# A list-scheduling planner for an FNet-plus-MLP kernel: a model of TensorE's half clock, unused products in planned gaps, and a table of urgencies for the work ahead of the MLP

## The chip, the cores and the metric

One core of a Trainium2 chip runs the kernel. The time is the device time of one execution in microseconds (us), the median of three runs. The profile is that of one further execution.

## The reference

The input x is 2048 tokens by 1024 channels (f32). With six rows sa, ca, ga, sb, cb, gb of 1024 values made from a condition vector (`silu(c) @ w_mod`):

```
h = layernorm(x) * (1 + ca) + sa
x = x + ga * Real(DFT_seq(DFT_hidden(h)))          # spectral part
h = layernorm(x) * (1 + cb) + sb
x = x + gb * (gelu(h_n @ w1 + b1) @ w2 + b2)       # h_n: h, layer-normalised again; w1 1024x3584, w2 3584x1024
```

The DFT matrices are inputs as well. Products must be good to f32, so operands are split into a high and a low f16 part and multiplied in three passes.

## The kernel before

**Spectral part.** The tokens are normalised in 16 tiles (`ln1`), transposed on TensorE (PE, L2740), and folded on VectorE (DVE: L2757 to L2827) with the symmetries of the DFT, which halves the products. ScalarE (ACT, L2833) and DVE (L2835) split the folded operand. The hidden transform is a set of units (`hid_unit`, PE L3060) for two classes of operands; ACT and DVE (L2586, L2589) split each result, and L2589 splits the sequence matrices too. The sequence transform runs over eight blocks b of 256 tokens (`seq_pair`): a product Q (PE L3136), evicted by ACT (L3140), and a product P (PE L3124), evicted by DVE in two halves (L3145, L3150).

**Per block, between the two parts** (`ln2`): DVE multiplies by ga (L3267), a DMA on GpSimd's (POOL) queue adds x from DRAM (L3277, L2180), ACT squares (L3241), DVE normalises (L3296, L3300), small DVE steps make a root (L2673 to L2676, L3307), ACT writes the normalised rows (L3309). Then `z_psum`: 20 transposes on PE (L3490), ACT and DVE split seven combinations into f16 (L3511, L3538), and ten small PE products (L3498) add or subtract earlier combinations in PSUM. L3538's results of blocks 4 and 5 go to DRAM on POOL's queue (L3530). Blocks 6 and 7 are "held": only L3267 is done at once, and the rest (`z_held`) during the MLP. There are 20 transposes and 10 products for each of the blocks 0 to 5.

**MLP.** Both weight products use a scheme with seven products in place of eight (Strassen-like), so a group is seven times 12 matmuls of 512 columns. The first product is L3962 (2352 matmuls in all), the second L4089 (2352). The first two groups of L3962 (`gemm3_first`, 168 matmuls) need only blocks 0 to 3, so they may stand between the last spectral steps. The weights are scaled and split on the fly by ACT (L2434) and DVE (L2447, L2461); `need` and `emitted` force what a group needs ahead of it.

**The planner.** Nothing is ordered by hand. The program is made of tasks, each with an engine, a cost in us and dependences, in streams; each stream has a due time. While the program is written, the planner keeps one clock for each engine, starts in each step the task that can start now and is due first (`pick_first`), and writes its instructions. So costs, lags (`LAGS`: from one engine's end to another's start), landing times of DMAs (`LANDS`) and due times settle the order on every engine, and the hardware then runs each engine's queue in that order. Up to the last combination of block 5 PE's products are planned too (`in_order`); after it PE's order is the MLP's fixed sequence, and the rest is placed around it. A PSUM bank is reused by a list of the tasks that last used it (`last`, `zlast`, `bank_used`).

Of the kernel before, what the change touches and what calls it, by code (L numbers as in the profile page):

```python
# [17 lines left out]
P = 128  # L18
# [1973 lines left out]
def fast(ctx, tc, x, cre, cim, dre, dim, w1, b1, w2, b2, c, wm, out):  # L1992
# [207 lines left out]
    LAGS = {"w": 2.0, "rowl": 1.0, "crawl": 0.5, "row": 0.2, "rowp": 3.0, "ld": 0.5, "z": 1.0, "s": 0.5, "u": 0.3, "op": 0.4, "comb": 0.3, "ln": 0.2}  # L2200

    LANDS = {"dma": 2.0, "st": 4.0, ("st", "d"): 7.0, ("st", "u"): 5.0, ("st", "s"): 4.0, ("st", "z"): 4.0, ("st", "xa"): 8.0}
# [11 lines left out]
    class Task:  # L2214
        def __init__(self, eng, cost, fn, deps=(), key=None):
# [3 lines left out]
            self.tag, self.due, self.lag = None, 0.0, LAT  # L2219

# [43 lines left out]

    def chain(*steps):
# [5 lines left out]

    def push(stream, tag, tasks, due=0.0):
        for t in tasks:
            t.tag, t.due, t.lag = tag, due, LAGS.get(f"{stream}l" if t.eng == "dma" else stream, LAGS.get(stream, LAT))
            streams.setdefault(f"st_{stream}" if t.eng == "st" else stream, deque()).append(t)
# [228 lines left out]
    def add(stream, eng, cost, fn, deps=(), key=None, due=0.0, tag=None):  # L2504
        t = Task(eng, cost, fn, deps, key)
        push(stream, tag or stream, [t], due)
# [91 lines left out]
    def mod_part(k):  # L2598
# [10 lines left out]
        add("modp", "pe", CP * (1 + (k == 0)), f, [("wm", k)], ("mp", k), 1.0)  # L2609
# [72 lines left out]
    def ln1(bt):  # L2682
# [50 lines left out]
        for j in range(2):  # L2733
            for ga_, gd_, base in ((0, 3, 0), (1, 2, 1)):
# [3 lines left out]
                def turn(g, bk, j=j):  # L2738
# [7 lines left out]
                    add("lnt", "pe", 0.55, lambda g=g, bk=bk, turn=turn: turn(g, bk), deps + last[s], None, due)  # L2746
# [18 lines left out]
    def special(cls):  # L2765
# [4 lines left out]
        for hb in range(2):  # L2770
# [5 lines left out]
            k = add("lnt", "pe", 0.6, turn, [("n", 8 * cls + 7), *last[s]], None, due)  # L2776
# [148 lines left out]
    def row(n, j):  # L2925
# [4 lines left out]
        for c_ in range(2):  # L2930
# [34 lines left out]
            add("rowp", "pe", 2 * CP, f, deps, ("wrr", m), due)  # L2965
# [74 lines left out]
    def hid_unit(tp, t, cls, c_):  # L3040
# [23 lines left out]
        bp = 1024 * s  # L3064
        deps += last[s]
        last[s] = [("hid", n)]
        due = 40.0 + 22.0 * cls
        key = add("hidp", "pe", 2.1, f, deps, ("hidp", n), due)
# [31 lines left out]
    def seq_pair(b):  # L3100
# [37 lines left out]
        add("seqp", "pe", 2.75, q_mm, ak[tp] + copk + bank_deps + ([("qs", b - 1)] if b else []), ("Q", b), due)  # L3138
        add("seqp", "pe", 3.0, p_mm, ak[tp] + copk + bank_deps + ([("y", b - 1)] if b else []), ("P", b), due)
        ev = lambda: act.activation(qv(b, 0, (257, 2), (1, 256)), PA(qb, (256, 2), (1, 256)), AF.Copy)  # L3140
        add("qs", "act", 0.65, ev, [("Q", b), ("qsz", b % 2)] + ([("y", b - 2)] if b > 1 else []), ("qs", b), due)
# [1312 lines left out]
```

## Time and profile before

| what | value |
|---|---|
| median of three runs | 1337.07 us (1335.74 to 1341.33) |
| the profiled execution: its time, its span | 1336.37 us, 1334.6 us |
| PE, DVE, ACT, POOL busy | 1228.5, 1058.8, 741.8, 253.9 us |
| mean granted clock of TensorE | 0.964 |
| first product of the MLP starts | 274.91 us |
| last combination of block 5 ends, from there on nothing but the MLP | about 305 us |

The span runs from the first instruction to the last; the run's own time is 1.8 us longer. PE busy counts a running matmul, at whatever clock; "granted clock" is 1 at full speed and 0.5 at half. A row of the timeline gives start, duration, engine, line, operation, output and inputs, and in brackets the engine's idle time before it with what ended it. `arena` is the one large SBUF tile and `ps` the eight PSUM banks, so most rows have the same names and go by their lines.

### The profile page before, as it was taken

How to read it: one execution, taken by the hardware profiler on the slowest of the kernel's cores; microseconds unless marked ns; L12 is line 12 of the kernel's file. 1: busy time of each engine (PE TensorE's matmuls, PEld its weight loads, DVE VectorE, ACT ScalarE, POOL GpSimd, SP SyncE). 2: the span in 40 equal slices, each digit the busy share in tenths (PEclk: the TensorE clock that was granted, in tenths of full speed). 3: DMA queues.
4: the chain of work that ended last, by engine and by line, in shares of the span. 5: the costliest groups of instructions: out<-in, count | busy, mean ns of one | idle time of the engine just before them, and what ended most of it. 6: DMA issues, size and time to landing. Idle time of an engine off the chain costs nothing.

```text
span 1334.6 us, 16823 instructions
## 1 busy us (share of the span) xinstructions
PE 1228.5 (92%) x5909; PEld 575.7 (43%) x5909; DVE 1058.8 (79%) x1602; ACT 741.8 (56%) x1194; POOL 253.9 (19%) x382
## 2 busy tenths in 40 slices
PE   3669796869999999999999999999999999999996
PEld 1225454534444444444444444444444444444442
DVE  5788688866888989989999986566777868585884
ACT  4875547766787585666746451466455554536330
POOL 2000033222000001000011101545233332233101
PEclk9779688889999999999999999999999999999998
DMA  9998378798436365543629696999585766575155
GB/s 364 402 298 268 111 244 214 173 262 278 170 113 231 107 247 175 196 156 111 251 89 291 162 394 170 292 271 331 200 298 176 270 240 190 199 280 195 60 177 114
DMA packets 105704, 292.59 MB, mean 219 GB/s; under 512 B 13340, under 2 KB 13356, under 8 KB 103688
## 3 DMA queue, kind: packets, MB, share of 16 engines
q1 hardware_dynamic: 77032, 198.26, 42.4%
q0 software_dynamic: 28576, 93.15, 24.3%
q8 instruction: 48, 0.79, 0.2%
q14 instruction: 48, 0.39, 0.1%
HBM read 205.37 MB, written 90.18 MB: 221 GB/s over the span
## 4 chain that ended last, share of the span: by engine, by line
PE 69%; DVE 6%; issue 2%; ACT 2%; DMA 1%; POOL 0%; SPq 0%; DVEq 0%; POOLq 0%
PE ps L3962 34%; PE ps L4089 34%; DVE arena L2447 2%; DVE arena L4141 1%; ACT arena L2434 1%; DMA fw<-arena 1%; DVE arena L2461 1%; DVE arena L3538 0%; DVE arena L3988 0%; ACT arena L3981 0%; PE ps L3387 0%; ACT arena L3511 0%; DVE arena L3296 0%; DVE arena L3375 0%; DVE arena L4196 0%
## 5 line engine op out<-in xcount | busy, mean ns | idle before, releaser
L3962 PE MATMUL ps<-arena 128*128 128x512 f16 x2352 | 514.6, 381 | 7.8 <-DVE arena L3150 6.6
L4089 PE MATMUL ps<-arena 128*128 128x512 f16 x2352 | 511.7, 379 | 5.9 <-DVE arena L4141 5.4
L3962 PEld LDWEIGHTS <-arena 128*128 128x128 f16 x2352 | 231.0, 98 | 287.9 <-issue 13.2
L4089 PEld LDWEIGHTS <-arena 128*128 128x128 f16 x2352 | 230.0, 98 | 284.4 <-issue 7.6
L4141 DVE SCALAR_TENSOR_TENSOR arena<-ps,i4c,arena 128x1024 f32<-128x1024 f32 x179 | 229.2, 1280 | 79.5 <-PE ps L4089 78.3
L2434 ACT ACTIVATE arena<-arena,shc 128x512 f16<-128x512 f32 (+1 forms) x115 | 116.2, 1016 | 119.4 <-DVE arena L2461 67.0
L2447 DVE SCALAR_TENSOR_TENSOR arena<-arena,shc 128x512 f16<-128x512 f32 (+1 forms) x115 | 128.9, 1121 | 39.1 <-ACT arena L2434 38.9
L3846 ACT ACTIVATE arena<-arena 128x512 f32<-128x512 f32 (+4 forms) x159 | 97.3, 613 | 111.7 <-DVE arena L3855 91.1
L2461 DVE TENSOR_TENSOR arena<-arena 128x512 f32<-128x512 f32 (+1 forms) x196 | 149.4, 764 | 4.0
L3981 ACT ACTIVATE arena<-arena,b1s,i1c 128x512 f32<-128x512 f32 x78 | 63.4, 813 | 86.4 <-DVE arena L3988 86.4
L2434 ACT ACTIVATE arena<-arena,s1c 128x512 f16<-128x512 f32 (+1 forms) x70 | 60.6, 886 | 65.2 <-DVE arena L2461 33.5
L3855 DVE TENSOR_TENSOR arena<-arena 128x256 f32<-128x256 f32 x240 | 88.4, 419 | 3.6 <-DMA arena<-in_cre_dram 3.0
L3988 DVE TENSOR_TENSOR arena<-arena,ps 128x512 f32<-128x512 f32 x78 | 53.3, 684 | 43.2 <-PE ps L3962 41.9
L3627 POOL PARTITION_ALL_REDUCE sums<-sums x21 | 11.5, 552 | 373.3 <-DVE sums L3623 355.2
L2447 DVE SCALAR_TENSOR_TENSOR arena<-arena,s1c 128x512 f16<-128x512 f32 (+1 forms) x70 | 65.9, 960 | 10.0 <-ACT arena L2434 9.6
L3984 ACT ACTIVATE arena<-ps 128x512 f32<-128x512 f32 x78 | 45.9, 589 | 39.0 <-PE ps L3962 38.7
L2447 DVE SCALAR_TENSOR_TENSOR arena<-arena,s2c 128x1024 f16<-128x1024 f32 x49 | 61.7, 1279 | 2.9 <-ACT arena L2434 2.8
L2434 ACT ACTIVATE arena<-arena,s2c 128x1024 f16<-128x1024 f32 x49 | 54.7, 1137 | 2.7 <-DVE arena L2461 1.7
L3060 PE MATMUL ps<-arena 128*128 128x256 f16 (+5 forms) x297 | 47.0, 310 | 8.3 <-ACT arena L2833 3.2
L3615 ACT ACTIVATE ps<-arena 128x1024 f32<-128x1024 f32 x46 | 46.8, 1018 | 9.1 <-DMA arena<-in_w_dram 4.7
L3892 POOL DMA_DIRECT2D arena<-in_cim_dram x69 | 38.1, 558 | 54.6 <-ACT arena L3846 26.4
L2740 PE MATMUL ps<-ident,arena 128*128 128x128 f32 x128 | 23.3, 329 | 25.1 <-POOL arena L2901 14.7
(259 smaller groups left out, 1137.8 us busy)
## 6 DMA issues: line engine op xcount, KB each, us to landing
fw<-arena SPq DMA_DIRECT2D x71, 512.0 KB, 4.4
arena<-fw SPq DMA_DIRECT2D x119, 256.0 KB, 3.8
arena<-fw SPq DMA_DIRECT2D x49, 512.0 KB, 5.9
arena<-in_wm_dram SPq DMA_DIRECT2D x32, 512.0 KB, 7.0
arena<-in_w_dram SPq DMA_DIRECT2D x32, 512.0 KB, 7.1
arena<-in_cre_dram POOLq DMA_DIRECT2D x64, 256.0 KB, 5.3
arena<-in_cim_dram POOLq DMA_DIRECT2D x64, 256.0 KB, 4.7
arena<-in_w_dram SPq DMA_DIRECT2D x56, 256.0 KB, 4.8
```

Of the source, the lines that this page charges most:

```text
L2434: act.activation(o[m][0], q(j), AF.Copy, **sc)
L2447: dve.scalar_tensor_tensor(o[m][1], q(j), scale, o[m][0], op0=ALU.mult, op1=ALU.subtract)
L2461: dve.tensor_tensor(q(d), q(a), q(b), op=op)
L3060: pe.matmul(PA(bp + o, (1, w), pn=m), l, r, start=i == 0, stop=i == len(mm_) - 1)
L3615: act.activation(junk, parts[j][0], AF.Square, accum_out=t[:, j : j + 1])
L3846: f = lambda: act.activation(v, v, AF.Square, accum_out=csum[0:pn, n : n + 1])
L3855: return lambda: dve.tensor_tensor(dst[0][:, o::2], src[0][:, o::2], dst[0][:, o::2], op=op)
L3962: pe.matmul(ps.rearrange("p (k t) -> p k t", k=4), w1at(g, m)[:, a, d * P : (d + 1) * P], zc(m)[:, b, :, d, :], start=(start and d == 0 an ...
L3981: act.activation(dst, src, AF.Gelu_apprx_tanh, scale=inv, bias=b1s[:, 2 * p + j : 2 * p + j + 1])
L3988: after_pe("dve", 0.6, lambda: dve.tensor_tensor(q, q, ps[b], op=ALU.add), kp[b])
L4089: pe.matmul(t[:, j], hidc[:, c_, m, a, k * P : (k + 1) * P], w2c[:, m, c_, w], start=(start and c_ == 0 and n == 0), stop=(c_ == 1 and n = ...
L4141: lambda: dve.scalar_tensor_tensor(dst, ps[b], inv, dst, op0=ALU.mult, op1=ALU.add), kp[b],
```

## The change

1. **PE's clock is modelled** (`pe_run`): time is cut into windows of 3.4133 us that begin at the planner's time 0. PE's work in a window counts; under 46% of it the next window runs at half speed, over 85%, or with three windows in a row over 60%, at full speed. The costs of PE's tasks are set to values for full speed.
2. **Unused products** (`keep_warm`): when the next planned PE task would start after a gap, and PE's idle time in the last window is over 0.8 us, the planner writes products of the identity with itself (128x128 by 128x256, f16) into a PSUM bank that no one uses at that time. `own`, `takes` and `gives` tell it which banks are free. From 45 us of planned time on; there are 195 of them: 58 in the transposes of `ln1`, 137 from the sequence transform on, none among the hidden units.
3. **Urgencies**: a table `DUES` replaces the due time of 17 pairs of stream and due time (two of the rows below); the planner's lags and landing times for PE are corrected.
4. The two held blocks are due 150 and 330 us into the MLP, before 200 and 350, and wait twice for their tasks at `gbb_rows`.

```diff
-    LAGS = {..., "rowp": 3.0, ...}
-    LANDS = {"dma": 2.0, ...}
+    LAGS = {..., "rowp": 0.4, ...}
+    LANDS = {"pe": 0.15, "dma": 2.0, ...}
...
         def run(self):
+            if self.eng == "pe" and in_order[0]:
+                keep_warm(self, self.start())
             t = self.start() + self.cost
+            if self.eng == "pe" and in_order[0]:
+                t = pe_run(self.start(), self.cost, 0.7 if self.tag == "hidp" else 1.0)
+            for k in self.takes:
+                spare.pop(k, None)
+            for k in self.gives:
+                spare[k] = t + LAT
...
+    TICK, PHASE = 3.4133, 0.0
+    pe_work, pe_state = {}, [0.5]
+    def pe_run(t, cost, weight):
+        while cost > 1e-9:
+            k = int((t - PHASE) // TICK) + 1
+            while len(pe_state) <= k:
+                w = pe_work.get(len(pe_state) - 1, 0.0) / TICK
+                n = len(pe_state)
+                up = w > 0.85 or min(pe_work.get(n - i, 0.0) for i in (1, 2, 3)) > 0.6 * TICK
+                pe_state.append(0.5 if w < 0.46 else 1.0 if up else pe_state[-1])
+            d = min(cost / pe_state[k], PHASE + k * TICK - t + 1e-6)
+            pe_work[k] = pe_work.get(k, 0.0) + weight * d
+            cost -= d * pe_state[k]
+            t += d
+            pe_spans.append((t - d, t))
+        return t
+    def keep_warm(task, start):
+        if KEEP is None or start < KEEP:
+            return
...
+        b = min(free, key=lambda k: free[k])
+        idle = TICK - sum(e - max(s, start - TICK) for s, e in pe_spans)
+        n = int(min(start - max(clk["pe"], free[b]) - 0.3, idle - IDLE) / 0.11)
...
+        for _ in range(n):
+            pe.matmul(PA(512 * b, (1, 256)), w[:, 0:P], w[:, 0 : 2 * P], start=True, stop=True)
+        clk["pe"] = pe_run(max(clk["pe"], free[b]), 0.11 * n, 1.0)
+    KEEP, IDLE = 45.0, 0.8
...
+    DUES = {
+        ("cop1h", 61.0): 34.4, ("doph", 26.0): 28.3, ("doph", 40.0): 36.0, ("fold0", 27.0): 22.1,
+        ("foldh0", 27.0): 63.8, ("hidh", 40.0): 14.8, ("i4", 29.558): 32.8, ("ln0", 144.0): 126.6,
...
-            t.tag, t.due, ... = tag, due, ...
+            t.tag, t.due, ... = tag, DUES.get((stream, due), due), ...
...
-        return due[3, 2] + 200.0 + 150.0 * v
+        return due[3, 2] + 150.0 + 180.0 * v
```

**PE, behind the last product P of block 7.** Rows L3124 (before) and L3188 (after) are P, L3962 the MLP's first product, L3563 the small products of `z_psum`, L3555 its transposes, L2313 the unused products. Lines of the changed kernel are 63 to 65 higher at these places. Before:

```order
L3124 LDWEIGHTS arena_65
L3124 MATMUL ps<-arena_65 128x256
L3962 LDWEIGHTS arena_65
L3962 MATMUL ps<-arena_65 128x512
...
L3490 MATMUL ps<-ident_107,arena_65 128x128 x20
L3498 LDWEIGHTS arena_65
L3498 MATMUL ps<-arena_65 128x512
```

and now:

```order
L3188 MATMUL ps<-arena_65 128x256
L3563 LDWEIGHTS arena_65
L3563 MATMUL ps<-arena_65 128x512
...
L2313 LDWEIGHTS ident_107
L2313 MATMUL ps<-ident_107 128x256
L3555 MATMUL ps<-ident_107,arena_65 128x128 x4
L2313 LDWEIGHTS ident_107
L2313 MATMUL ps<-ident_107 128x256
```

Four L3563 of block 3, 3 unused products, block 4's transposes with 15 more unused ones among them, 7 more, and block 4's first six L3563 now stand ahead of the MLP's first product. Ahead of block 5's last small products (four L3563) stand 96 of the MLP's matmuls in place of 36: 12, then 60 before block 5's transposes, then 12 and 12. Between the last of them and the first L4089 stand 156 matmuls in place of 216.

**DVE, around block 7's eviction (L3145 and L3150, now L3210 and L3215).** `lns_24` are block 4's statistics, `lns_25` block 5's, `csum` those of the held blocks; L3296 (now L3361) and L3267 (now L3332) are steps of `ln2`. Before:

```order
L3296 SCALAR_TENSOR_TENSOR arena_65<-arena_65,lns_25_167 128x1024
L3538 TENSOR_TENSOR arena_65<-ps,arena_65 128x2x512
...
L3300 SCALAR_TENSOR_TENSOR arena_65,lns_24_166<-arena_65,lns_24_166 128x1024 x2
L3296 SCALAR_TENSOR_TENSOR arena_65<-arena_65,lns_25_167 128x1024
L3288 SCALAR_TENSOR_TENSOR csum_160<-csum_160 128x2
L3145 TENSOR_TENSOR arena_65<-ps,arena_65 128x2x256
L3150 TENSOR_TENSOR arena_65<-ps,arena_65 128x2x257
```

and now:

```order
L3332 SCALAR_TENSOR_TENSOR arena_65,lns_25_167<-arena_65 128x1024
L3353 SCALAR_TENSOR_TENSOR lns_25_167<-lns_25_167,csum_160 128x2
L3210 TENSOR_TENSOR arena_65<-ps,arena_65 128x2x256
L3603 TENSOR_TENSOR arena_65<-ps,arena_65 128x2x512
L3332 SCALAR_TENSOR_TENSOR arena_65,csum_160<-arena_65 128x1024
L3215 TENSOR_TENSOR arena_65<-ps,arena_65 128x2x257
L3603 TENSOR_TENSOR arena_65<-ps,arena_65 128x2x512
L3603 TENSOR_TENSOR arena_65<-ps,arena_65 128x512
L3332 SCALAR_TENSOR_TENSOR arena_65,csum_160<-arena_65 128x1024
L3353 SCALAR_TENSOR_TENSOR csum_160<-csum_160 128x2
L3603 TENSOR_TENSOR arena_65<-ps,arena_65 128x2x512
L3361 SCALAR_TENSOR_TENSOR arena_65<-arena_65,lns_25_167 128x1024 x2
```

Block 4's normalisation is now finished before block 7's eviction, and block 5's two L3296 come behind it, as do block 4's combinations (L3603, before L3538).

**POOL, the stores of the combinations (L3530, now L3595).** `fzc_67` to `fzc_73` are the DRAM buffers of the seven combinations, first block 4's and then block 5's; L2183 and L3271 (now L3336) add the held blocks and others to the output, and the ISA row is a sum over partitions that the MLP's weight scale waits for. Before:

```order
L3530 DMA fzc_68<-arena_65 256x1x512
L2183 DMA out_dram<-arena_65,idxm_108 1024x1024
L3530 DMA fzc_72<-arena_65 256x1x512
L3530 DMA fzc_70<-arena_65 256x1x512
L3271 DMA out_dram<-arena_65 128x1024
L3530 DMA fzc_71<-arena_65 256x1x512
L3530 DMA fzc_73<-arena_65 256x1x512
L3530 DMA fzc_69<-arena_65 256x1x512
L3627 ISA sums_2032<-sums_2032 128x1
L3530 DMA fzc_67<-arena_65 256x1x512
```

and now:

```order
L3595 DMA fzc_68<-arena_65 256x1x512
L3595 DMA fzc_72<-arena_65 256x1x512
L3595 DMA fzc_70<-arena_65 256x1x512
L3595 DMA fzc_71<-arena_65 256x1x512
L3336 DMA out_dram<-arena_65 128x1024
L3595 DMA fzc_73<-arena_65 256x1x512
L3595 DMA fzc_69<-arena_65 256x1x512
L2183 DMA out_dram<-arena_65,idxm_108 1024x1024
L3336 DMA out_dram<-arena_65 128x1024
L3595 DMA fzc_67<-arena_65 256x1x512
L3692 ISA sums_2224<-sums_2224 128x1
```

Block 4's first five stores are no longer parted by the held blocks' additions, and these stand before block 5's.

More of the change, by code (lines that the diff above doesn't have):

```diff
@@ L2263, in run @@
             self.fn()
+    TICK, PHASE = 3.4133, 0.0
[14 more added lines that the diff above has]
+        return t
+    pe_spans = deque()
+    def keep_warm(task, start):
+        if KEEP is None or start < KEEP:
+            return
+        while pe_spans and pe_spans[0][1] < start - TICK:
+            pe_spans.popleft()
+        free = dict(spare)
+        if task.own:
+            free[task.own[0]] = max([0.0] + [done[d] + LAT for d in task.own[1] if d is not None])
+        if not free:
+            return
+        b = min(free, key=lambda k: free[k])
+        idle = TICK - sum(e - max(s, start - TICK) for s, e in pe_spans)
+        n = int(min(start - max(clk["pe"], free[b]) - 0.3, idle - IDLE) / 0.11)
+        if n <= 0:
+            return
+        w = ident.bitcast(F16) if hasattr(ident, "bitcast") else ident[:, :].bitcast(F16)
+        for _ in range(n):
+            pe.matmul(PA(512 * b, (1, 256)), w[:, 0:P], w[:, 0 : 2 * P], start=True, stop=True)
+        clk["pe"] = pe_run(max(clk["pe"], free[b]), 0.11 * n, 1.0)
+    spare = {}
+    KEEP, IDLE = 45.0, 0.8
     def chain(*steps):
@@ L3064, in hid_unit @@
         bp = 1024 * s
+        own = 2 * s, tuple(last[s])
         deps += last[s]
@@ L4347, in gbb_rows @@
         need("n2_0")
-        need(*(f"z{b}" for b in HELD))
+        for _ in range(2):
+            need(*(f"z{b}" for b in HELD))
         t = at(20, 1024)
```

48 lines of the change are left out of this document (28 added, 20 removed).

## The prediction

> **What bounds the kernel now.** I read the page's slices first (the granted clock in 40 parts of 33 us each), then the engines' busy time by stage, then PE's timeline at the seams.
>
> ```profile
> PEclk9779688889999999999999999999999999999998
> ```
>
> ```profile
> core 0: us, PE busy (x) PEld busy (x) DVE busy (x) ACT busy (x) POOL busy (x), PEclk, DMA share, GB/s
> 0.00:305.00 305.00, 215.73 (x1209) 115.60 (x1210) 236.79 (x416) 195.77 (x309) 53.55 (x89) 0.85 0.80 259
> 139.00:172.00 33.00, 31.02 (x150) 15.76 (x151) 21.60 (x35) 16.70 (x25) 1.36 (x5) 0.68 0.41 144
> 142.00:146.00 4.00, 4.00 (x19) 1.87 (x18) 2.73 (x3) 2.01 (x2) 0.00 (x0) 0.50 0.00 0
> 146.00:150.00 4.00, 4.00 (x20) 2.14 (x19) 3.31 (x4) 3.91 (x5) 0.00 (x0) 0.54 0.00 0
> 158.00:162.00 4.00, 2.37 (x12) 1.24 (x12) 3.90 (x10) 0.00 (x0) 0.00 (x0) 0.74 0.94 326
> 162.00:166.00 4.00, 4.00 (x19) 1.74 (x18) 2.17 (x5) 2.31 (x4) 0.23 (x1) 0.50 0.95 313
> 274.91:305.04 30.13, 22.06 (x97) 10.72 (x97) 15.82 (x38) 20.19 (x29) 9.50 (x12) 0.87 0.89 263
> 305.04:1324.80 1019.76, 1012.73 (x4701) 460.14 (x4699) 821.23 (x1185) 545.97 (x886) 200.38 (x293) 1.00 0.64 208
> ```
>
> The kernel has two halves. From 305.04 to 1324.80 us PE is busy for 1012.73 of 1019.76 us at clock 1.00: there only fewer products help. Ahead of it PE is busy for 215.73 of 305 us at clock 0.85, DVE for 236.79, the DMA share is 0.80: no engine is full, and the end is set by waits between them. PE's timeline shows the seam:
>
> ```profile
> 265.49 2.81 PE L3124 MATMUL ps<-arena 128*128 128x257 f16 x24
> 274.91 4.96 PE L3962 MATMUL ps<-arena 128*128 128x512 f16 x12 [6.61 <-DVE arena L3150]
> ...
> 304.39 0.81 PE L3498 MATMUL ps<-arena 128*128 128x512 f16 x3 [1.17 <-DVE arena L3538]
> 305.04 46.78 PE L3962 MATMUL ps<-arena 128*128 128x512 f16 x216
> 351.65 36.42 PE L4089 MATMUL ps<-arena 128*128 128x512 f16 x168
> ```
>
> I call S the end of block 5's last small products (L3498), 305.04 us. Behind S stand 216 products L3962 without a gap, then the first L4089. All waits of PE for L4089 behind S together, and the tail behind the last product, are small:
>
> ```profile
> PE ps L4089 <- DVE arena L4141: 5.4, 5, 1.8
> ```
>
> ```profile
> 1325.14 1.09 SPq L4136 DMA_DIRECT2D out_dram<-arena  x2
> ```
>
> So the time is S (305.04) + 1019.76 + 9.8 to the span's end (1334.6) + 1.77 outside it = 1336.37 us, the profiled execution; the median is 0.70 above it. A change pays if it brings S sooner, or puts more of the MLP ahead of S.
>
> **The change part by part.**
>
> *60 products go ahead of S.* 96 MLP products stand there in place of 36, 156 behind S in place of 216. One costs (351.65 − 305.04)/216 = 0.2158 us, 60 cost 12.95. They are free where they fill PE's waiting: from 274.91 to 305.04 PE is idle for 30.13 − 22.06 = 8.1 us, and for 6.6 more just before. That is 14.7 of idle time for 12.95 of work: enough, barely. Term **−12.95**, if S itself stays; the other terms are S's own.
>
> *The last stretch.* DVE's timeline:
>
> ```profile
> 272.30 1.28 DVE L3296 SCALAR_TENSOR_TENSOR arena<-arena,lns 128x1024 f32<-128x1024 f32 x1
> 273.50 0.15 DVE L3288 SCALAR_TENSOR_TENSOR csum<-csum 128x2 f32<-128x2 f32 x1
> 273.57 0.69 DVE L3145 TENSOR_TENSOR arena<-ps,arena 128x512 f32<-128x512 f32 x1
> ...
> 302.42 0.15 DVE L3631 TENSOR_SCALAR sums<-sums 128x1 f32<-128x1 f32 x1 [5.89 <-POOL sums L3627]
> ...
> 306.35 1.23 DVE L3538 TENSOR_TENSOR arena<-ps,arena 128x1024 f16<-128x1024 f32 x1 [1.94 <-ACT arena L3511]
> ...
> 347.28 1.28 DVE L2447 SCALAR_TENSOR_TENSOR arena<-arena,s2c 128x1024 f16<-128x1024 f32 x1
> ```
>
> and ACT's row beside it, the held blocks' L3267, and the landing time of x on POOL's queue:
>
> ```profile
> 301.77 1.02 ACT L3511 ACTIVATE arena<-ps 128x1024 f16<-128x1024 f32 x1 [5.43 <-DMA fzc<-arena]
> ```
>
> ```profile
> L3267 DVE SCALAR_TENSOR_TENSOR arena<-arena 128x1024 f32<-128x1024 f32 x14 | 17.1, 1219 | 0.1
> ```
>
> ```profile
> arena<-in_x_dram POOLq DMA_DIRECT2D x5, 512.0 KB, 7.4
> ```
>
> Until 302 both DVE and ACT wait for POOL's queue (5.89 and 5.43, the same time): the sum over partitions and block 4's stores stand behind the held blocks' additions. In the new order five of block 4's stores come first. I let 5.9 go. Two more L4299, of 512 columns like L3145, stand ahead of S: +1.4. Block 5's x now comes late: its two L3296 stand behind five steps of 1.22 us, three of 0.69 and two of 0.15 = 8.5 us after its L3267, while x needs 7.4 to land and two squares on ACT (1.02 by ACT's row of the same width): some 2 us of new wait on DVE, with block 5's chain and the held blocks' L3267 behind it. −5.9 + 1.4 + 2 = **−2.5**; bounds −5.9 and +2 (the POOL wait stays, and the new one comes).
>
> On DVE two L3296, two of the held L3267 and three combinations (2.6 + 2.4 + 3.1 = 8 us) leave the place ahead of block 7's eviction for behind it. Block 7's last P is done at 268.3 and DVE comes at 273.57, so the eviction may come up to 5.3 sooner, which pays for most of that. I count this at zero.
>
> *The hidden stage.* DVE's steps ahead of L2835, which splits the second class, and PE's rows there:
>
> ```profile
> 128.78 5.01 DVE L2827 TENSOR_TENSOR arena<-arena 128x1024 f32<-128x1024 f32 x4
> 133.71 1.29 DVE L2589 SCALAR_TENSOR_TENSOR arena<-ps,arena 128x513 f16<-128x513 f32 x2
> ```
>
> ```profile
> 135.86 0.46 PE L3060 MATMUL ps<-arena 128*128 128x257 f16 x2 [3.23 <-ACT arena L2833]
> 139.10 11.26 PE L3060 MATMUL ps<-arena 128*128 128x257 f16 x49 [2.78 <-DVE arena L2835]
> ...
> 159.63 8.37 PE L3060 MATMUL ps<-arena 128*128 128x257 f16 x36 [1.88 <-DVE arena L2589]
> ```
>
> In the new order two of the four L2827 (2.5) and two L2589 (1.3) stand behind L2835: PE's restart at 139.10 comes **−3.8** sooner. If that closes the gap the clock may stay up as well: 31.02 us busy at clock 0.68 is 21.1 at full speed, 9.9 less; bounds 0 and −13.7. No unused product stands among the hidden units, and PE waited 3.23 and 2.78 us in a row there, so I don't take the 9.9.
>
> What the clock does shows in the windows: PE starts at 139.10, yet the clock is 0.50 until 146 and 0.54 until 150, so some 10 us of work were needed. And an idle of 1.88 us, at 157.75, was enough to lose it: 0.74, then 0.50.
>
> The Trainium skill, "TensorE: Matmul & The Clock Gate" ("What's actually happening"), lets one busy window of about 3.4 us bring full speed, with windows that run freely. By that the restart at 139.10 would cost about 1.7 us where the rows show some 5; the rows decide, since I only take the idle time here.
>
> *Unused products.* A product of this width costs 2.81/24 = 0.117 us warm and 11.26/49 = 0.230 cold. 195 of them are 22.8 to 44.8 us of PE, against 305 − 215.73 = 89 us of idle time. Where the plan errs, due work stands behind them. What they can save shows here:
>
> ```profile
> 203.90 4.68 PE L3124 MATMUL ps<-arena 65*128 65x257 f16 x26 [3.44 <-DVE arena L3150]
> 208.43 2.35 PE L3490 MATMUL ps<-ident,arena 128*128 128x128 f32 x20
> ...
> 228.25 4.03 PE L3490 MATMUL ps<-ident,arena 128*128 128x128 f32 x20 [5.14 <-ACT arena L3309]
> ```
>
> 20 transposes took 4.03 behind a wait of 5.14 and 2.35 warm: 1.7 lost. 26 P took 4.68, and 26 × 0.117 = 3.04 warm: 1.6. Two or three such places lie on the chain, 3 to 5 us. Against it, a quarter of the 195 late and warm is 5.7. Term **0**; bounds −5 and +22.8.
>
> *First L4089.* Its weights have to be scaled and split (L2447, L2461) behind S. Before, DVE works from 306.35 to 348.5 on these, 42.1 us, with 46.6 to spend; now 156 × 0.2158 = 33.7. What is missing is 8.4 at most; DVE also fits weight work for later groups into that time, so part can move: **+2**, bounds 0 and +8.4.
>
> *Held blocks* (150 and 330): their transposes run in the MLP, where PE has 7.0 us of idle time in all and DVE 821 of 1020 busy; **0**, within a few us, and the second wait at `gbb_rows` with it.
>
> Sum: 1336.37 − 12.95 − 2.5 − 3.8 + 0 + 2 = 1319.1; with 0.70 to the median, **1320 us**.
>
> **The rivals.**
>
> *The first L4089 waits in full*: the 42.1 us can't be pressed into 33.7; DVE is busy at that place nearly without a gap, which speaks for it. +8.4 in place of +2: 1326.
>
> *The hidden stage stays warm*: for it, the idle time at 136 to 139 goes; against, the wait of 1.88 at 157.75 was enough to lose the clock. −9.9 more: 1310.
>
> *S goes later by about as much as moves ahead of it.* Block 5's last L3296 ended at 273.5, ahead of L3145 of block 7; now it ends 8.5 − 0.15 + 2 × 1.28 = 10.9 us behind that point. If block 7's eviction doesn't come sooner and the other gains of S are lost with it, S is at 316, and the 60 products fill a new wait: −12.95 + 11 + 2 = 0, so 1337. Against it: P of block 7 was ready 5.3 us before DVE.
>
> *Slower: the 137 unused products from the sequence stage on come late and cold.* They stand in PE's queue ahead of due work, planned by a clock of windows that start at the planner's 0. If they begin late, all of them at 0.23 push the chain by 31.5: 1351. It decides from 103 of 137 on, (1343.8 − 1320)/0.23. For it: PE ran cold just in those stretches. Against it: PE idled there for waits of 3 to 7 us, which swallow 13 to 30 cold products each.
>
> The Trainium skill, same page ("Why this matters for your kernels"), asks only that PE have no idle gaps over some 3 us; by that, unused products in shorter gaps buy nothing and are pure cost, which speaks for this rival. The trace lost the clock after 1.88 us, so here the row speaks against the rule.
>
> **How the numbers follow.** Forecast (1313 to 1325) 0.44; first L4089 in full 0.15; warm hidden stage 0.13; S later 0.17; late unused products 0.11. About 0.5%, 6.7 us, is what a measurement can tell from no change: 1330.4 and 1343.8. Faster is 0.44 + 0.15 + 0.13 = 0.72, same 0.17, slower 0.11. The range leaves the slower case out, and of the others little: from 1304 (the warm stage with 5 of the unused products' saving) to 1339 (S later, with the 2 us of POOL's wait in doubt).
>
> **What would show it.** In the profile after: S near 298, with 96 products L3962 (now L4027) ahead of it; from S to the last product 1019.76 − 12.95 + 2 = 1009 us; the first L4089 (now L4154) waits at most 3 us; no wait of DVE for POOL's sum over 2 us; PE's restart after class one near 135, and a clock still about 0.7 in that stage; transposes in the sequence stage at 2.4 us per 20. The forecast is wrong if S is at 309 or later, if PE waits over 6 us at the first L4154, or if rows of unused products (L2313) end while the operand of the next due product has long been ready.

## The result, and the profile after

The changed kernel takes 1347.59 us (median of 14 runs, 1338.51 to 1355.21) where the one before takes 1337.07: ratio 1.0062, 95% interval 1.0042 to 1.0082. (The ratios in this document are estimated from all executions of both kernels; that of the two medians would be 1.0079.) The change is slower by 0.6%; forecast were 1320 us. The profiled execution took 1348.03 us (span 1346.1), 11.66 more than that of before. Lines of the changed kernel are 62 to 65 higher than before's at the places named here: L4027 is the MLP's first product, L4154 its second, L3563 the small products, L2496 ACT's split of a weight.

The slices and PE's seam, to hold against those of before:

```profile
PEclk9679699998999999999998999999999999999999
```

```profile
306.15 2.75 PE L4027 MATMUL ps<-arena 128*128 128x512 f16 x12
308.74 1.03 PE L3563 MATMUL ps<-arena 128*128 128x512 f16 x4
309.61 7.93 PE L4027 MATMUL ps<-arena 128*128 128x512 f16 x36
322.45 28.28 PE L4027 MATMUL ps<-arena 128*128 128x512 f16 x120 [4.91 <-ACT arena L4359]
350.57 36.42 PE L4154 MATMUL ps<-arena 128*128 128x512 f16 x168
```

The 156 products stand behind S as the order said, but S is at 309.77 (before 305.20, both to the end of the last L3563 or L3498), and 36 products later PE stands for 4.91 us. PE's waits for products of the MLP behind 300 us are 21 us, before 7 (5.4 for L4141, 1.2 and 0.4 for two others):

```profile
PE ps L4027 <- ACT arena L4049: 8.4, 2, 6.7
PE ps L4154 <- DVE arena L4206: 7.6, 7, 1.9
PE ps L4027 <- ACT arena L4359: 4.9, 1, 4.9
PE ps L4154 <- DVE arena L2509: 0.4, 1, 0.4
```

By stage, from the starts and ends of the same steps in both traces (Q: first product of the sequence transform; P: end of block 7's last P). The third column is another execution of the changed kernel (run e0 below), of which more at once:

| stage, us | before | after | after, e0 |
|---|---|---|---|
| start to Q | 167.93 | 172.56 | 166.57 |
| Q to P | 100.37 | 97.07 | 94.63 |
| P to S | 36.90 | 40.14 | 38.49 |
| S to the first second-layer product | 46.45 | 40.80 | 42.80 |
| from there to the last product | 973.15 | 986.17 | 985.79 |

The last row holds the most: 13 us lost in the middle of the MLP, where I had put nothing. Three rows of PE say where most of it is, behind a wait of 6.65 us for ACT and then 60 products at 16.06 us, which take 13.11 elsewhere:

```profile
699.75 10.52 PE L4027 MATMUL ps<-arena 128*128 128x512 f16 x48
716.92 16.06 PE L4027 MATMUL ps<-arena 128*128 128x512 f16 x60 [6.65 <-ACT arena L4049]
732.82 5.34 PE L4154 MATMUL ps<-arena 128*128 128x512 f16 x24
```

ACT's rows ahead of it, in e0 at the same place (PE's wait there is 6.66, until 708.84). L3490 is a combination of held block 7:

```profile
699.12 1.14 ACT L2496 ACTIVATE arena<-arena,s2c 128x1024 f16<-128x1024 f32 x1
700.16 1.14 ACT L2496 ACTIVATE arena<-arena,s1c 128x1024 f16<-128x1024 f32 x1
703.50 2.19 ACT L2496 ACTIVATE arena<-arena,s2c 128x1024 f16<-128x1024 f32 x2 [2.20 <-DVE arena L2523]
705.59 0.71 ACT L2496 ACTIVATE arena<-arena,s1c 128x512 f16<-128x512 f32 x1
706.20 0.62 ACT L3490 ACTIVATE arena<-arena 128x512 f16<-128x512 f32 x1
707.15 1.15 ACT L2496 ACTIVATE arena<-arena,s1c 128x1024 f16<-128x1024 f32 x1 [0.34 <-DVE arena L2523]
708.21 0.58 ACT L4049 ACTIVATE arena<-ps 128x512 f32<-128x512 f32 x1
```

On ACT, L4049, which frees a PSUM bank for PE, stands behind six splits of weights, with two waits for DVE among them, and behind the held block's combination.

The wait of 4.91 us is followed back in the chain of waits (a start, a duration, who):

```profile
304.17 0.42 POOL out_dram L2183
304.58 0.63 issue
305.22 10.71 DMA out_dram<-arena
315.93 0.02 SPq L3867
315.95 0.03 issue
315.99 4.76 DMA arena<-in_w_dram
320.74 0.02 issue
320.77 1.15 ACT arena L2496
321.91 0.49 ACT arena L4359
```

The held blocks' addition to the output left POOL at 305, landed 10.71 us later, and only then might SP load a second-layer weight into its place. ACT's L2496 waited for that weight, the eviction L4359 stood behind it on ACT, and PE behind the eviction.

And the hidden stage. SP's queue and the DMA engines 70 to 95 us, ACT and PE 50 us later:

```profile
70.59 2.46 SPq L2978 DMA_DIRECT2D out_dram<-in_x_dram  x3
89.45 0.81 SPq L3012 DMA_DIRECT2D arena<-in_wm_dram  x2
90.35 1.40 SPq L2948 DMA_DIRECT2D arena<-in_cre_dram  x2
```

```profile
80.00:90.00 10.00, 6.39 (x38) 1.89 (x39) 8.47 (x17) 8.92 (x13) 0.00 (x0) 0.60 0.07 26
```

```profile
126.92 1.06 ACT L3680 ACTIVATE arena<-arena 128x1024 f16<-128x1024 f32 x1 [4.80 <-DMA arena<-in_w_dram]
```

```profile
129.32 8.65 PE L3123 MATMUL ps<-arena 128*128 128x257 f16 x36 [2.29 <-DVE arena L2652]
137.90 3.64 PE L3019 MATMUL ps<-arena,scol 128*32 128x512 f32 x16
147.81 13.93 PE L3123 MATMUL ps<-arena 128*128 128x257 f16 x66 [6.27 <-DVE arena L2652]
```

Two loads of the condition rows' weights stand on SP ahead of the DFT matrix's loads, and wait until 89.45 for PE's row products; the DMA engines are busy 7% of 80 to 90 us. Before, the share there was 0.94:

```profile
80.00:90.00 10.00, 7.53 (x27) 2.51 (x26) 9.27 (x17) 10.00 (x18) 0.35 (x1) 0.50 0.94 239
```

The weight that ACT's L3680 squares, behind all these loads on SP, is late; the hidden units' evictions stand behind L3680 on ACT; PE waits 2.29 us, runs the next 36 products at 0.24 us each, and comes to its second class at 147.81 (before 139.10).

### The profile page after: what moved, and what is told of

It is laid out like the page before. It is cut to its first block, busy times and chain, and to the rows that moved or that the text cites. A ratio compares the mean times of both kernels' runs of the same rounds, so it can differ in the third digit from the quotient of the medians.

```text
span 1346.1 us, 17222 instructions
## 1 busy us (share of the span) xinstructions
PE 1246.7 (93%) x6104; PEld 591.4 (44%) x6104; DVE 1058.2 (79%) x1602; ACT 741.8 (55%) x1194; POOL 253.3 (19%) x382
## 4 chain that ended last, share of the span: by engine, by line
PE 69%; DVE 11%; DMA 9%; ACT 5%; issue 4%; POOL 1%; SPq 0%; DVEq 0%; POOLq 0%; ACTq 0%
PE ps L4154 34%; PE ps L4027 30%; DMA arena<-in_wm_dram 2%; DVE arena L2509 2%; ACT arena L2496 2%; DMA arena<-in_w_dram 2%; DVE arena L4206 1%; PE ps L3123 1%; DMA arena<-in_cim_dram 1%; DMA arena<-in_x_dram 1%; DVE arena L2523 1%; PE ps L3188 1%; DMA out_dram<-arena 1%; ACT arena L2649 1%; DVE arena L3603 1%
## 5 line engine op out<-in xcount | busy, mean ns | idle before, releaser
L4027 PE MATMUL ps<-arena 128*128 128x512 f16 x2352 | 518.2, 382 | 17.4 <-ACT arena L4359 9.0
L4154 PE MATMUL ps<-arena 128*128 128x512 f16 x2352 | 512.0, 379 | 8.2 <-DVE arena L4206 7.6
L4027 PEld LDWEIGHTS <-arena 128*128 128x128 f16 x2352 | 231.7, 99 | 300.7 <-issue 22.9
L4154 PEld LDWEIGHTS <-arena 128*128 128x128 f16 x2352 | 229.9, 98 | 286.4 <-issue 7.8
L4206 DVE SCALAR_TENSOR_TENSOR arena<-ps,i4c,arena 128x1024 f32<-128x1024 f32 x179 | 229.3, 1281 | 76.2 <-PE ps L4154 74.4
L2496 ACT ACTIVATE arena<-arena,shc 128x512 f16<-128x512 f32 (+1 forms) x115 | 116.3, 1016 | 119.0 <-DVE arena L2523 65.9
L2496 ACT ACTIVATE arena<-arena,s1c 128x512 f16<-128x512 f32 (+1 forms) x70 | 60.6, 885 | 66.0 <-DVE s1c L3709 34.6
L3692 POOL PARTITION_ALL_REDUCE sums<-sums x21 | 12.6, 602 | 362.2 <-DVE sums L3688 354.8
L4049 ACT ACTIVATE arena<-ps 128x512 f32<-128x512 f32 x78 | 45.9, 588 | 36.1 <-PE ps L4027 35.9
L2496 ACT ACTIVATE arena<-arena,s2c 128x1024 f16<-128x1024 f32 x49 | 54.9, 1138 | 13.3 <-DMA arena<-in_w_dram 6.8
L3680 ACT ACTIVATE ps<-arena 128x1024 f32<-128x1024 f32 x46 | 46.8, 1017 | 6.7 <-issue 3.6
L3957 POOL DMA_DIRECT2D arena<-in_cre_dram x69 | 38.9, 578 | 39.9 <-ACT arena L3911 18.5
```

Of the source, the lines that this page charges most:

```text
L2496: act.activation(o[m][0], q(j), AF.Copy, **sc)
L3957: return lambda t: gp.dma_start(t[0:pn], v)
L4027: pe.matmul(ps.rearrange("p (k t) -> p k t", k=4), w1at(g, m)[:, a, d * P : (d + 1) * P], zc(m)[:, b, :, d, :], start=(start and d == 0 an ...
L4154: pe.matmul(t[:, j], hidc[:, c_, m, a, k * P : (k + 1) * P], w2c[:, m, c_, w], start=(start and c_ == 0 and n == 0), stop=(c_ == 1 and n = ...
L4206: lambda: dve.scalar_tensor_tensor(dst, ps[b], inv, dst, op0=ALU.mult, op1=ALU.add), kp[b],
```

## The experiments

Fourteen runs; the kernel before ran beside each on the same chip, and ratios are against it. e1 to e5 ran on one chip, e0 and e6 to e8 on a second, e9 to e11 on the first again, so that medians of runs from different sets are best held against each other by their ratios. The last three runs are single executions, on a third chip. The change also holds one dependence that the list in "The change" leaves out (DVE's `hid_scale(0)` waits for the last of the tasks `bt_` as well); no run parts it from the rest. The moved steps go through one helper in the planner, which holds a step's instructions back until another step has written its own, and changes neither the plan nor any other order (it shifts lines by 11):

```diff
+    MOVED = {...}
+    behind = {}
+    def emit(task):
+        if task.key in MOVED:
+            behind.setdefault(MOVED[task.key], []).append(task.fn)
+            return
+        task.fn()
+        for f in behind.pop(task.key, ()):
+            f()
...
-            self.fn()
+            emit(self)
```

| run | median us | ratio to before (95%) | profiled: Q, S, S to second layer, from there to the end |
|---|---|---|---|
| e0, the change itself | 1347.99 | 1.0060 (1.0036 to 1.0085) | 166.57, 299.69, 42.80, 985.79 |
| e1, no unused products | 1340.07 | 1.0016 (0.9999 to 1.0033) | 167.46, 302.09, 41.14, 985.75 |
| e2, loads moved | 1341.77 | 1.0023 (1.0004 to 1.0043) | 163.72, 296.37, 42.66, 987.46 |
| e4, stores moved | 1341.27 | 1.0020 (1.0004 to 1.0036) | 167.00, 299.88, 38.87, 993.30 |
| e5, held at 200 and 350 | 1341.72 | 1.0037 (1.0019 to 1.0054) | 166.64, 299.49, 42.86, 987.59 |
| e6, held at 110 and 310 | 1336.96 | 0.9981 (0.9962 to 1.0000) | 166.39, 299.61, 42.87, 980.25 |
| e11, e6 and loads | 1330.84 | 0.9932 (0.9910 to 0.9953) | 164.54, 299.74, 42.80, 979.12 |
| e7, e11 and stores | 1326.20 | 0.9911 (0.9886 to 0.9935) | 165.80, 298.62, 37.11, 981.04 |
| e8, e7 and squares | 1327.70 | 0.9923 (0.9900 to 0.9947) | 163.38, 301.58, 33.51, 978.96 |
| e9, e7, no unused products | 1328.15 | 0.9914 (0.9893 to 0.9934) | 164.60, 300.13, 34.69, 978.95 |
| e10, e6 without the table | 1341.77 | 1.0021 (1.0003 to 1.0039) | 173.69, 314.05, 35.49, 980.73 |

**e1: without the unused products.**

```diff
-        for _ in range(n):
-            pe.matmul(PA(512 * b, (1, 256)), w[:, 0:P], w[:, 0 : 2 * P], start=True, stop=True)
         clk["pe"] = pe_run(max(clk["pe"], free[b]), 0.11 * n, 1.0)
```

> The changed kernel without the 195 unused products; every other instruction stands in the same order. Theory Q (what the two traces suggest: the time is lost in queues in which something waits ahead of due work; SP's in the first 120 us, POOL's at 285 to 316): the unused products are not the loss, they even pay in the sequence stage, where 20 transposes took 2.35 to 2.66 us instead of 4.03. Without them the clock falls there again: +1 to +5 us against the changed kernel's 1347.6, so 1348 to 1353. Rival F (the fourth rival of the prediction: unused products late and cold ahead of due work): 5 to 20 us faster, 1328 to 1342.

Measured 1340.07: below the range of the one and inside that of the other, by the median. The profile speaks against F all the same: Q to P is 97.20 us against 94.63 with them in e0, and S comes 2.4 us later. Between Q and P the granted clock is at half for 3.4 us in e0 and for 13.7 us in e1. The gain is not there in every execution: with the unused products ten of twelve profiles have 94.4 to 95.3 us from Q to P, but the profile after has 97.07 and e11 97.17; without them e1 has 97.20 and e9 96.71. The same 20 transposes, first in the profile after, then in e0's and then in e1's (whose lines are 2 lower):

```profile
232.49 2.66 PE L3555 MATMUL ps<-ident,arena 128*128 128x128 f32 x20 [2.41 <-ACT arena L3374]
```

```profile
225.57 4.07 PE L3555 MATMUL ps<-ident,arena 128*128 128x128 f32 x20 [2.41 <-ACT arena L3374]
```

```profile
229.03 4.53 PE L3553 MATMUL ps<-ident,arena 128*128 128x128 f32 x20 [4.92 <-ACT arena L3372]
```

They halve PE's idle time here, from 4.92 to 2.41 us. Whether the clock then stays up is another matter: it did in the profile after and in e11 (2.66 us each), and did not in the ten others with unused products (3.64 to 4.07 us). Why e1's median is lower than e0's is not shown by this run. e9 asks the same with the loads moved.

**e2: two loads moved on SP's queue.** `MOVED = {('wr', 16): ('cr', 5), ('wr', 17): ('cr', 5)}`.

> The changed kernel with two loads of the condition rows' weights (512 KB each) moved on SP's queue behind the eight loads of the DFT matrix that stood behind them; nothing else moves. Theory Q: those two loads wait for PE's row products until 89.4 us and hold SP, so the DMA engines stand still from 80 to 90 us (share 0.07) and the weight loads that ACT's squares wait for (4.80 us at 122) come some 6 us late. Moved, the DMA share at 80 to 90 rises above 0.8, ACT's wait falls below 2 us, PE stays warm longer in the hidden stage, and the first product of the sequence stage comes 5 to 9 us before its 172.56 us: 1339 to 1343. Rival F: nothing changes, 1346 to 1349.

Measured 1341.77. In its profile the DMA share of 80 to 90 us is 0.65, not above 0.8 but far from 0.07; ACT's wait for the weight is 0.79 us, and Q is at 163.72. Q comes 2.9 us sooner than in e0 and S 3.3 us; but from S to the last product it takes 1030.1 us against 1028.6. Theory Q holds, but for the size of the DMA share.

**e4: two stores moved on POOL's queue.** `MOVED = {('st', 'z', (4, 5)): ('st', 'xo', 14), ('st', 'z', (4, 6)): ('st', 'xo', 14)}`.

> The changed kernel with two of block 4's stores moved on POOL's queue behind block 7's two additions to the output; nothing else moves. Theory Q: these additions went out at 304 to 305 us, so the weight load into the same SBUF place could start only at 316, ACT's L2496 waited 6.83 us for it with PE's eviction behind it, and PE stood for 4.91 us and then ran cold. Moved, the additions go out before 301, the load before 312, PE's wait for L4359 falls below 2 us and the cold stretch at 320 to 330 goes: 4 to 8 us faster, 1340 to 1344. Rival F: nothing changes, 1346 to 1349. Rival D (the DMA engines are full there, share 0.95, so the order of the queue doesn't matter): the load lands no sooner, 1346 to 1349.

Measured 1341.27. The addition leaves POOL at 292.55, against 295.35 in e5 with the stores where they were and S at the same place (299.9 and 299.5). It still takes 10.78 us to land; the load starts 3.7 us sooner, and PE's wait for L4359 is 3.5 us against 6.7, and the second layer starts 4 us sooner after S. So the order of the queue does matter, but rival D has a share: the landing takes long in either order (10.7 us in the profile after, 11.1 in e0, 11.7 in e5). In this execution the 4 us are lost again later, at a wait of 7.2 us for DVE's L4217 (L4206 of the change).

**e5: the old due times.** `due[3, 2] + 200.0 + 150.0 * v`.

> The changed kernel with the held blocks due at 200 and 350 us again (the second wait at gbb_rows stays). The order up to the MLP is the same; inside the MLP the held transposes stand 12 and 48 products later. Theory H (the new due times of the held blocks put block 7's combinations where weights are needed: PE's wait of 6.65 us and cold products behind it near 717 us): that wait goes, 6 to 10 us faster, 1338 to 1342. Theory Q (the waits ahead of 330 us decide; the place of the held blocks matters little): 1344 to 1350, and a wait of some us for L4049 stays.

Measured 1341.72, and the wait is not gone but longer: 12.5 us in two waits for L4049, the longest 11.3. So it isn't the due times as numbers; the transposes stand at 984 and 1764 products, where before they stood at 696 and 1500 with the same due times. What the planner knows of the rest of the MLP has moved too. The time lies in theory H's range, but not for its reason.

**e0: the change itself, beside the next three.**

> The changed kernel, unaltered, beside the three below on the same chip. In the four runs so far, three of which leave everything ahead of the sequence transform as the change made it or nearly so, that transform began at 166.6 to 167.5 us and block 5's last small product ended at 299.5 to 302.1; in the first profile of the changed kernel at 172.56 and 309.8. Theory V (the first profile caught a late weight load, which differs from execution to execution): here the transform begins near 167 and the time is 1340 to 1343. Rival: the first profile is the rule and each of the three edits was worth 5 us by itself: 1346 to 1349.

Its profiled execution took 1339.24, its median is 1347.99: the profile is theory V's (0.8 us below its range), the median the rival's. Seven of its 12 executions lie between 1347 and 1357, five between 1339 and 1342; e12 to e14 ask why. A median of two such groups moves with the size of the groups: e5 has seven executions between 1339 and 1342 and five between 1345 and 1348, so its lower group is e0's, and the 6 us between the two medians are no proof of a gain.

**e6: the held blocks where they stood before.** `due[3, 2] + 110.0 + 200.0 * v`, chosen by the order: 720 and 1500 matmuls.

> The changed kernel with the held blocks due at 110 and 310 us, chosen so that their transposes stand behind the same products of the MLP as in the kernel before (720 and 1500 matmuls, before 696 and 1500; the change has 972 and 1716). Nothing ahead of the MLP moves. Theory H (where the held blocks' combinations fall decides; at the change's place they keep ACT and DVE from evicting, PE waits 6.6 us for L4049 and runs cold after it): that wait is under 2 us, and from the first second-layer product to the last it takes 973 to 977 us as before, not 986: 8 to 13 us less, 1328 to 1334. Rival (the wait comes from the weights, wherever the held blocks stand): a wait of 5 to 7 us for L4049 stays, 1339 to 1343.

Measured 1336.96, 11 us below e0 on the same chip; the profiles are 5.5 us apart, and the ratios 0.9981 and 1.0060. PE's waits from the first second-layer product on are now these; the 6.7 is gone, and one wait of 4.3 at 499 us has come:

```profile
PE ps L4154 <- DVE arena L4206: 8.7, 5, 4.3
PE ps L4027 <- ACT arena L4049: 3.2, 3, 2.2
PE ps L4154 <- DVE arena L2509: 0.4, 1, 0.4
```

That stretch takes 980.25, not 973 to 977, and the median is above theory H's 1328 to 1334: its mechanism stands, with 5.5 of the 12.6 us back, its sizes do not. The other 7 us are in these waits (8.7 us for L4206 and 3.2 for L4049, before 5.4 and 1.2) and in 3.4 us at half clock behind the one at 499 us. What brings them is open; that 96 products ahead of S shift the weights' work against the held blocks would be a reason, but no run shows it.

**e7, e8 and e11: the moves together.** e11 is e6 with e2's move, e7 has e4's as well, e8 moves three squares on ACT besides (`864`, `865` and `866` behind `('root', 5)`).

> e6 with the two loads of e2 moved on SP's queue and the two stores of e4 moved on POOL's. Theory H with theory Q: each works on another stage, so the gains add: another 2 to 5 us less than e6, 1325 to 1331, with block 5's last small product near 296. Rival (slack: what is gained ahead of the MLP is waited for behind it, since the weights of the second layer come by the time of the held blocks' additions): within 1.5 us of e6.

> e7 without the move of the two stores on POOL's queue (the held blocks at 110 and 310, the loads on SP's queue moved). It parts e7's gain over e6 (10.8 us between the medians, 6.0 between the profiles). Theory B (ACT's wait for the late load stands on the brink of costing PE its clock, so e6's executions fall into two groups, and moving the loads removes the slower one): most of the gain is here, 1328 to 1331, and the runs lie within 6 us of each other. Rival (POOL's stores carry it): 1333 to 1337.

> e7 with three of ACT's squares of a second-layer weight, which wait for their load at 276 to 283 us, moved behind block 5's second statistics. Theory Q: DVE's wait of 3.2 us for L2730 goes and block 5's last small product comes 3 to 4 us sooner (near 292); the time falls by 1 to 3 us against e7. Rival (slack, as above): the S comes sooner but the time is within 1.5 us of e7.

e11 is 0.5% below e6 and its six executions lie within 4 us: theory B. e7 is another 0.2% below, which the two intervals don't part, but its second layer starts 5.7 us sooner after S (37.11 against 42.80); S is at 298.62, not near 296. Its 1326.20 beats the kernel before by 0.9%, and is the best of all. In e8 PE no longer waits for L4370 (L4359 of the change), yet the time is e7's within the intervals: DVE's wait for the statistics stays (3.62 us, in e7 3.18), S is 3 us later, not sooner, and the next stage 3.6 shorter. That is the rival's slack: what S gains or loses there is made up at the weights of the second layer.

**e9: e7 without the unused products.**

> e7 without its 195 unused products, all else in the same order. Theory W (they pay a little: in e1's profile, without them, the sequence stage took 97.2 us against 94.6 with them): the sequence stage is 2 to 3 us longer and the time 1 to 4 us above e7's 1326.2, so 1327 to 1330. Rival F (late and cold; e1's median was below that of the changed kernel): 2 to 6 us below e7, 1320 to 1324.

0.9914 against 0.9911: no difference that the intervals could tell. Q to P takes 96.71 against 94.61 in e7, so in these two profiles 2.1 us are saved where they stand, and S to the second layer is 2.4 us longer with them. Saved, and waited for 40 us later. Theory W is right in the stage and wrong in the sum; F falls.

**e10: e6 without the table.** `DUES = {}`.

> e6 with the table of urgencies emptied: the clock model, the new costs and the unused products stay (179 of them), the held blocks stand at the same places as in e6, and 96 MLP products stand ahead of block 5's last small products, as in e6. Theory M (the model and the costs carry the 96 products and the sequence stage; the table only shifts steps by a few us): within 4 us of e6's 1336.96, so 1333 to 1341. Rival T (the table is what brings block 5 forward): its last small product comes at 305 or later and the time is 1343 or more.

Between the two: 1.0021 against e6's 0.9981, so the table (it has 18 pairs, not 17) is worth some 0.4%. S is 14.4 us later than in e6, 7.3 of it at Q already, but S to the second layer takes 35.49 in place of 42.87. 96 products stand ahead of S in both. So they come without the table, from the costs, the lags and the model, which no run parts; and half of what the table gains at S is lost at the same weights.

**e12, e13, e14: three more executions of the change.**

> One more profiled execution of the changed kernel, unaltered, to see what its slower executions do. Theory B (the brink): the execution's time follows the hidden stage. Where ACT's longest wait for the weight load at 121 to 127 us is over 4.5 us, PE's wait at 127 to 130 goes over 2 us, the next 18 or 36 products run cold (0.24 us each), the sequence transform begins at 171 or later and the time is 1346 or more; else it begins near 167 and the time is 1338 to 1342. Rival: the time differs by over 5 us between executions whose sequence transform begins at the same time; then the slower group comes from a later stage.

> As e12: a further execution of the changed kernel, with the same two outcomes.

> As e12: a further execution of the changed kernel, with the same two outcomes.

Measured 1339.35, 1346.32 and 1340.29, with Q at 165.71, 171.25 and 166.39. With the two profiles there were, five executions: three at 1339 to 1340 with Q at 165.7 to 166.6, two at 1346 and 1348 with Q at 171.3 and 172.6. They part at one wait. PE in e12, and then in e13:

```profile
126.74 2.46 PE L3123 MATMUL ps<-arena 128*128 128x257 f16 x18 [1.08 <-DVE arena L2652]
129.99 2.45 PE L3123 MATMUL ps<-arena 128*128 128x257 f16 x18 [0.79 <-DVE arena L2652]
132.37 1.92 PE L3019 MATMUL ps<-arena,scol 128*32 128x512 f32 x16
```

```profile
128.83 8.50 PE L3123 MATMUL ps<-arena 128*128 128x257 f16 x36 [2.03 <-DVE arena L2652]
137.26 2.89 PE L3019 MATMUL ps<-arena,scol 128*32 128x512 f32 x16
```

The same 36 products and 16 row products end at 134.3 in the one and at 140.2 in the other. Theory B holds in all five, two of which were known when it was written.

The two groups part earlier still, at the clock. In every profile of this case the granted clock changes only at points that lie whole multiples of 3.41 us apart, and where these points fall differs from execution to execution. In e13 and in the profile after they fall alike, and the clock is at half from 71.0 to 88.1 us; in e0, e12 and e14 it is at half from 72.1 to 72.7 until 85.7 to 86.4. In that stretch run the 32 row products for which SP's two loads wait, in e12 and then in e13:

```profile
82.29 5.32 PE L3019 MATMUL ps<-arena,scol 128*32 128x512 f32 x32 [5.55 <-ACT arena L3041]
```

```profile
83.32 5.97 PE L3019 MATMUL ps<-arena,scol 128*32 128x512 f32 x32 [6.58 <-ACT arena L3041]
```

So the loads leave SP at 89.31 and 89.45 in the slower two, at 87.63 to 88.51 in the other three, and ACT's wait for the weight ends at 126.44 and 126.92 against 124.34 to 125.18. PE's idle time then falls almost whole between two such points, 125.6 and 129.0, with PE busy for 1.4 of 3.41 us, and at 129.0 the clock goes to half. e1, e4, e5 and e6, whose queues in this stage are the change's but for e1's unused products, go with the faster three (half until 86.1 to 87.0, loads at 87.90 to 88.57, Q at 166.39 to 167.46). This fits all nine profiles, but no run sets where the points fall, so that they make the two groups is argued, not shown.

It doesn't explain all of the table. e4 moves nothing ahead of 285 us and e1 nothing but unused products, and yet only one of their 24 executions is above 1345; and of the executions at 1350 to 1356 there is no profile. What sets the share of the slower executions is open; e1 to e5 ran on another chip than e0, and that alone was not tried.

## Why the prediction was wrong, point by point

The steps that failed are the held blocks, put at nothing and 12.6 us in the runs, the hidden stage, where a gain of 3.8 us was counted and anything from 2.2 us of gain to 4.6 of loss came, and the first second-layer product, whose weights took back 9 us where 2 were allowed. By the prediction's own sum, on the execution that e0 shows, since the three faster profiles agree closely: 1319.1 + 2.4 (hidden) − 5.7 (Q to P) + 4.1 (P to S) + 7.3 (first second-layer product) + 12.6 (held blocks) − 0.6 (tail) = 1339.2. The two slower profiles take 7 to 9 us more, 5 to 6 of it by Q.

- *60 products, −12.95.* Right: 96 stand ahead of S, and S in e0 is at 299.7 where I had 298. S itself was right in three profiles of five, and by luck: a gain of 5.7 us from Q to P, for which I had no term, paid for what the next two terms missed.
- *Hidden stage, −3.8.* Failed. I counted DVE's four steps that move, and didn't look at what stands ahead of them on ACT, nor at SP's queue, whose two condition loads move ahead of eight others; the order showed both. Q comes 1.4 to 2.2 us sooner in the three faster profiles, 3.3 to 4.6 later in the two slower ones. e2 and e11, with the two loads moved back, have it at 163.72 and 164.54, 4.2 and 3.4 sooner than before.
- *Last stretch, −2.5.* The parts came as I had them, the sum did not: P to S takes 1.6 us longer in e0, not 2.5 less. DVE's wait of 5.89 for POOL's sum is 1.9 in e0 and gone in the profile after, and the new wait for block 5's x is there, 1.84 us for an estimate of 2 (with both squares counted, my figures give 7.4 + 2 × 1.02 − 8.5 = 0.9, so the agreement is luck). What I hadn't seen is ACT: three squares of weights that wait for their loads stand ahead of block 5's second statistics, and DVE waits 3.78 us for these.

```profile
281.45 2.48 DVE L3361 SCALAR_TENSOR_TENSOR arena<-arena,lns 128x1024 f32<-128x1024 f32 x2 [1.84 <-ACT arena L3306]
...
295.13 0.17 DVE L2736 RECIPROCAL lns<-lns 128x2 f32<-128x2 f32 x1 [3.78 <-ACT lns L2730]
```

- *Unused products, 0.* Right, and for half the reason: in most profiles they save 2.1 to 2.6 us in their stage, as I had it, and lose them at the second layer's weights (e7 against e9), not by being late. The 2.4 us that I expected for 20 transposes came for some blocks only (4.07 above).
- *Q to P, no term.* 5.7 us are saved there, 2.6 of them by the unused products if e1's profile is held against e0's; the rest I left out, and no run says what it comes from.
- *First L4089, +2.* The size is near my upper bound (+8.4; measured 42.8 − 33.7 = 9.1), the mechanism is not mine. Not DVE's 42 us of splitting: a weight's load waits for the place that the held blocks' addition leaves, and that addition leaves POOL no sooner than before (293.38 before, 295.35 in e5, 297.35 in e0), though S is 5.5 us sooner. PE's wait behind it is 7.6 of the 9.1 us in e0; with the additions moved ahead e4 has 4 us back, and in e8, where the wait is gone, the stage takes 33.51.
- *Held blocks, 0 within a few us.* Failed, and by the most: 12.6 us, of which e6 has 5.5 back by the places alone. I argued from idle shares (DVE 821 of 1020 us busy). The order showed their transposes moving from 696 and 1500 products to 972 and 1716, and I didn't ask what ACT and DVE have to do at the new places.
- *Rivals.* "S goes later" did not come true: in the slower executions S is at 304.6 and 309.8, not at 316, and by the hidden stage, not by block 7's eviction. "Late unused products" gave the right side for the wrong cause. No rival had a queue of ACT's in the MLP.

## What to carry to other kernels

When work is moved ahead of a bottleneck, the gain is real only if everything behind the bottleneck comes sooner too: here S gained 5.5 us and 60 products, and the weights of the next stage, loaded into places that other work frees at its old time, took back 9 us of it, and the middle of the MLP, where the held blocks have new places, lost 12.6. So follow, for each step that a new order moves, the queue in which it stands (a load on SP that waits for a buffer holds all loads behind it; a split on ACT that waits for its load holds the evictions behind it), and do this for the places in the steady part as well, where shares of busy time say nothing of a wait of 7 us. Here three moves (the held blocks, two loads, two stores) turned 1.006 into 0.991. And a model of the clock is no better than its time 0: the planner lets the windows begin there, while in the traces it differs from execution to execution where they begin.

## What the runs showed of the hardware

The granted clock goes down or up only at points that are whole multiples of 3.41 us apart, in all sixteen profiles, and where these points lie differs from execution to execution. So the length of an idle time alone doesn't tell what it costs. The idle time of 2.41 us ahead of the 20 transposes shown under e1 lies between two such points in e0 (222.6 and 226.0), and the clock is at half from 226.0 to 229.5; in the profile after, one of the points (231.4) cuts it, and the clock stays up until 238.2. In the hidden stage idle times of 1.88 us (before) and 2.03 us (e13) lay between two points and lost the clock, 2.29 us (after) almost so. A cut one of 1.52 us (e6) left it up, and so did a cut one of 1.75 us (e1):

```profile
127.41 2.45 PE L3123 MATMUL ps<-arena 128*128 128x257 f16 x18 [1.52 <-DVE arena L2652]
```

```profile
128.48 2.45 PE L3121 MATMUL ps<-arena 128*128 128x257 f16 x18 [1.75 <-DVE arena L2650]
```

The Trainium skill, "TensorE: Matmul & The Clock Gate" ("Why this matters for your kernels"), warns of gaps over some 3 us; in these traces 1.88 and 2.03 us were enough.
